# Moving both halves of the expert block's input by 32 bytes in SBUF

## The chip, the core and the metric

The kernel runs on one core of one Trainium2 chip. The metric is the device time of one execution in microseconds (us), lower is better. Before the change three runs took 735.52, 736.44 and 738.17 us; their median, 736.44 us, is what the changed kernel is compared with.

## The reference

Attention with a narrow window feeds a gated feed-forward block. Cut to what matters:

```python
batch, n_heads, seq, head_dim = (4, 8, 768, 64)
n_tokens, d_model, d_ff = (3072, 512, 1536)

scores = scale * q @ k.T - slope[h] * dist       # kept: 8 global columns, 96 local ones
a = softmax(where(keep, scores, -1e9))
x = (a @ v).transpose(0, 2, 1, 3).reshape(B * S, H * D)      # 3072 x 512
gate = 1.0 / (1.0 + np.exp(-(x @ w_gate)))
val = x @ w_val
return (gate * val @ w_out).astype(np.float32)
```

All of it is float32 in and float32 out.

## The kernel before, in words

**Tiling.** The 3072 tokens are cut into 8 blocks of 384 (three tiles of 128). For each block the kernel first makes x, transposed, with the 512 model dimensions on 4 x 128 partitions and the 384 tokens along the free dimension. Then it goes through the 12 slices of 128 hidden units (`seq`, line 631): `ff_in` (line 554) multiplies x by a slice of w_gate and of w_val, and `ff_out` (line 588) multiplies the result by the matching 128 rows of w_out and adds into three PSUM banks.

**Two halves.** TensorE multiplies here in a rounded 32-bit form (float32r). To keep float32 accuracy, each operand is split into a high half, which is the value rounded to that form, and a low half, which is the rest; a product is then three matmuls (low x high, high x low, high x high). x is kept as `xh` and `xl`, the first-layer weights as `w1h` and `w1l`, the second-layer weights as `w2h` and `w2l`, the hidden values as `hh` and `hl`.

**The matmuls that read x.** In `ff_in`, line 564, the weights are the stationary operand and x is the moving one:

```python
for wt, xt in ((w1l, xh), (w1h, xl), (w1h, xh)):
    nc.tensor.matmul(
        ps[:, :n], wt[f][:, i, c], xt[:, c, :n], start=(k == 0), stop=(k == 3 * NC - 1)
    )
```

That is 2 (gate, value) x 4 (chunks `c` of 128 dimensions) x 3 = 24 matmuls of 128 x 384 for one slice, and with 12 slices and 8 blocks 2304 in all. In `ff_out`, line 604, the hidden values are stationary and `w2l` or `w2h` is moving: 9 matmuls of 128 x 512 for one slice. The first six slices of the first block do `ff_out` in plain float32 instead.

**Who writes x.** `pair_out` (line 515) writes x for one pair of heads: for the first block three pairs by GpSimd (lines 540 and 541, the latter recorded under line 180, the helper `sub`), everything else by ScalarE (`xh`, line 544) and VectorE (`xl`, line 545). Each of `xh` and `xl` holds two blocks, one being read while the next is written.

**Order.** The attention of later blocks is cut into events (line 632) that are placed by hand between the slices of the expert block, so TensorE gets its attention work (lines 387 and 502) between `ff_in` and `ff_out`. A few orders are fixed by hand with `issue_after` (line 62). Nothing there names x's address.

**Where tiles lie.** A pool lays its tiles one behind the other in each partition, every tile rounded up to 32 bytes, and pools lie one behind the other in the order in which they are made (lines 45 to 50: wpool, cpool, xpool, small, mpool, w2pool). In the kernel before, counted in bytes from the start of a partition:

```
tile                          pool     starts at   modulo 64
w1h, w1l (24 tiles)           wpool    1152 ...    0
ident                         cpool    124128      32
xh                            xpool    131616      32
xl                            xpool    143904      32
sums, rcs, sm, rc, top, flag  small    156192 ...  32 and 0 in turn
gnm, gsm, grc                 small    156640 ...  32, 0, 32
work, hl, hh                  mpool    156736 ...  0
w2h, w2l                      w2pool   171072 ...  0
kr, pT, qs, ks                inner    175168 ...  0
```

The chunks of `xh` and `xl` lie 1536 bytes apart (384 x 4) and their two blocks 6144 bytes, both multiples of 64, so every slice of x that a matmul reads begins at 32 modulo 64.

**The branch that is not taken.** `dense_block` (line 794) is a general path for other values of n_global and n_local or for rows that don't fit; at the end a flag decides (`redo`, line 843), and line 845 runs in its place when it isn't needed. `gnm`, `gsm` and `grc` are used there alone.

Of the kernel before, what the change touches and what calls it, by code (L numbers as in the profile page):

```python
# [8 lines left out]
F32 = mybir.dt.float32  # L9
# [10 lines left out]
P = 128  # L20
# [8 lines left out]
def attn_moe_kernel(ctx, tc, qT, kT, v, n_global, n_local, wg, wv, wo, out, B, H, S, D):  # L29
# [17 lines left out]
    xpool = ctx.enter_context(tc.tile_pool(name="xpool", bufs=1))  # L47
    small = ctx.enter_context(tc.tile_pool(name="small", bufs=4))
# [218 lines left out]

    PAIR = 1
    blocks = [(b, t0, TB) for b in range(B) for t0 in range(0, NTB, TB)]
    xall = [xpool.tile([P, 2 * NC * NB], F32R, name=name) for name in ("xh", "xl")]  # L270
    xslot = {}
    offs = 0
# [496 lines left out]
    def dense_tables(t):  # L769
        reli = gpool.tile([P, S], I32, name="reli")  # L770
        nc.gpsimd.iota(reli, pattern=[[-1, S]], base=t * P, channel_multiplier=1)
        rel = gpool.tile([P, S], F32, name="rel")
        nc.vector.tensor_copy(rel, reli)
        keep = gpool.tile([P, S], F32, name="keep")
        pen = gpool.tile([P, S], F32, name="pen")
        dist = gpool.tile([P, S], F32, name="dist")
        nc.vector.tensor_scalar(keep, rel, nf[:, 0:1], None, op0=ALU.is_lt)
        nc.vector.tensor_scalar(pen, rel, 0.0, None, op0=ALU.is_ge)
        nc.vector.tensor_tensor(keep, keep, pen, op=ALU.mult)
        nc.gpsimd.iota(reli, pattern=[[1, S]], base=0, channel_multiplier=0)  # L780
        glo = gpool.tile([P, S], F32, name="glo")
        nc.vector.tensor_copy(glo, reli)
        nc.vector.tensor_scalar(glo, glo, nf[:, 1:2], None, op0=ALU.is_lt)
        nc.vector.tensor_tensor(pen, glo, keep, op=ALU.mult)
        nc.vector.tensor_tensor(glo, glo, pen, op=ALU.subtract)

        nc.vector.tensor_tensor(dist, rel, keep, op=ALU.mult)
        nc.vector.tensor_scalar(pen, glo, nf[:, 0:1], None, op0=ALU.mult)
        nc.vector.tensor_tensor(dist, dist, pen, op=ALU.add)
        nc.vector.tensor_tensor(keep, keep, glo, op=ALU.add)  # L790
        nc.vector.tensor_scalar(pen, keep, 1.0, 1.0e9, op0=ALU.subtract, op1=ALU.mult)
        return keep, pen, dist

    def dense_block(b, t0, xh, xl):
        for t in range(TB):
            keep, pen, dist = dense_tables(t0 + t)
            for s in range(NPAIR):
                r0 = b * (H * D) + 2 * s * D
                qg = gpool.tile([P, P], F32, name="qg")
                nc.sync.dma_start(qg, qT[bass.ds(r0, P), (t0 + t) * P:(t0 + t + 1) * P])  # L800
                kg = gpool.tile([P, S], F32, name="kg")
                nc.sync.dma_start(kg, kT[bass.ds(r0, P), :])
                vg = gpool.tile([P, NTB, P], F32, name="vg")
                nc.sync.dma_start(
                    vg, v[bass.ds(b * S, S), s * P:(s + 1) * P].rearrange("(t p) x -> p t x", p=P)
                )
                nc.vector.tensor_scalar(qg, qg, SCALE, None, op0=ALU.mult)
                av = ps_a.tile([P, 4 * P], F32, name="ps_v")
                for j in range(2):
                    hd = slice(j * D, (j + 1) * D)  # L810
                    sb = gpool.tile([P, S], F32, name="sb")
                    for c in range(S // NB):
                        cols = slice(c * NB, (c + 1) * NB)
                        ps = ps_gv.tile([P, NB], F32, name=("ps_g", "ps_u")[c % 2])
                        nc.tensor.matmul(ps, qg[hd], kg[hd, cols], start=True, stop=True)
                        nc.vector.scalar_tensor_tensor(
                            sb[:, cols], dist[:, cols], -slopes[2 * s + j], ps, op0=ALU.mult, op1=ALU.add
                        )
                    nc.vector.tensor_tensor(sb, sb, keep, op=ALU.mult)
                    nc.vector.tensor_tensor(sb, sb, pen, op=ALU.add)  # L820
                    nm = small.tile([P, 1], F32, name="gnm", bufs=1)
                    nc.vector.tensor_reduce(nm, sb, axis=AX.X, op=ALU.max, negate=True)
                    sm = small.tile([P, 1], F32, name="gsm", bufs=1)
                    nc.scalar.activation(sb, sb, AF.Exp, bias=nm, accum_out=sm)
                    nc.vector.tensor_scalar(sm, sm, 1e-9, None, op0=ALU.add)
                    rc = small.tile([P, 1], F32, name="grc", bufs=1)
                    nc.vector.reciprocal(rc, sm)
                    nc.vector.tensor_scalar(sb, sb, rc, None, op0=ALU.mult)
                    pT = gpool.tile([P, NTB, P], F32, name="gpT")
                    for c0 in range(0, NTB, 3):  # L830
                        pt = ps_a.tile([P, 4, P], F32, name="ps_t")
                        for c in range(3):
                            nc.tensor.transpose(pt[:, c], sb[:, (c0 + c) * P:(c0 + c + 1) * P], ident)
                        nc.scalar.copy(pT[:, c0:c0 + 3], pt[:, 0:3])
                    for c in range(NTB):
                        nc.tensor.matmul(
                            av[hd, 0:P], vg[:, c, hd], pT[:, c], start=(c == 0), stop=(c == NTB - 1)
                        )
                cols = slice(t * P, (t + 1) * P)
                nc.scalar.activation(xh[:, s, cols], av[:, 0:P], AF.Copy)  # L840
                nc.vector.tensor_tensor(xl[:, s, cols], av[:, 0:P], xh[:, s, cols], op=ALU.subtract)
# [4 lines left out]
    with fits.Else():  # L846
        with tc.For_i(0, B, 1) as b:
            for t0 in range(0, NTB, TB):
                blocks.append((b, t0, TB))
                bi = len(blocks) - 1  # L850
                xslot[bi] = (0, NC * NB)
                dense_block(b, t0, *x_of(bi))
                for f in range(NF):
                    split_w2(f)
                    ff_in(bi, f)
                    ff_out(bi, f)
# [39 lines left out]
```

## Time and profile before

| | |
|---|---|
| median of 3 runs (lowest to highest) | 736.44 us (735.52 to 738.17) |
| span of the profiled execution, first to last instruction | 734.4 us |
| matmul (PE) busy | 718.1 us, 98% of the span |
| weight loads (PEld) busy, beside the matmuls | 653.0 us, 89% |
| VectorE (DVE) / ScalarE (ACT) / GpSimd (POOL) busy | 498.8 / 420.2 / 219.4 us |
| mean granted TensorE clock | 0.998 of full speed |

The profile's time is a span from the first to the last instruction of one execution; the runs' times are measured around the whole execution, so the span is the smaller number (734.4 us against a median of 736.44 us). Busy times of the engines overlap. Matmuls are pipelined: the duration of one record (336 ns at the median for a matmul on x) is longer than the step from its start to the next one's start, and successive records overlap. The rate is read from starts, not from durations.

### The profile page before, as it was taken

To read this page: it belongs to the slowest core of one execution; us is meant where nothing else is said; L and a number is where in the kernel's file an instruction comes from. 1 tells how busy PE (TensorE), PEld (TensorE's weight loads), DVE (VectorE), ACT (ScalarE), POOL (GpSimd) and SP (SyncE) were. 2 spreads that over 40 slices of the span, in tenths; PEclk is the share of its full clock that TensorE was granted. 3 is DMA by queue.
4 is the path that set the end of the run, shared out by engine and by line. 5 is a ranking of instruction groups with operands and counts; after the bars stand their busy time and mean duration, and the time that the engine had idled before them with its cause. 6 is when DMAs were issued, how large, how long until landed. Compare 5 with 4: busy or idle time off the path is not lost. (4 is left out here: it accounts for less than half of the span.)

```text
span 734.4 us, 12477 instructions
## 1 busy us (share of the span) xinstructions
PE 718.1 (98%) x4403; PEld 653.0 (89%) x4403; DVE 498.8 (68%) x1303; ACT 420.2 (57%) x948; POOL 219.4 (30%) x166
## 2 busy tenths in 40 slices
PE   7999999999999999999999999999999999999996
PEld 5667788999889999999999999999999999999996
DVE  7889799668877777686777868666786877321111
ACT  5789887656565555566456655655555664332222
POOL 5424345422231323223132332313233231221222
PEclk9999999999999999999999999999999999999999
DMA  8969662624437353433435442343435224010001
GB/s 249 275 194 274 189 199 59 167 61 81 106 79 159 85 106 71 100 103 68 79 80 121 110 106 63 65 122 74 96 81 110 72 47 83 16 45 1 1 0 46
DMA packets 136866, 74.27 MB, mean 101 GB/s; under 512 B 87136, under 2 KB 129120, under 8 KB 136800
## 3 DMA queue, kind: packets, MB, share of 16 engines
q1 hardware_dynamic: 136800, 73.43, 40.1%
q8 instruction: 36, 0.59, 0.3%
q14 instruction: 30, 0.25, 0.1%
HBM read 49.81 MB, written 6.29 MB: 76 GB/s over the span
## 5 line engine op out<-in xcount | busy, mean ns | idle before, releaser
L180 POOL TENSOR_TENSOR w2l<-w2f,w2h 128x512 fp32r<-128x512 f32 x89 | 122.5, 1377 | 372.8 <-ACT w2h L217 359.1
L581 DVE SCALAR_TENSOR_TENSOR work<-work,ps_u 128x384 f32<-128x384 f32 x90 | 49.8, 553 | 127.1 <-PE ps_u L564 122.1
L564 PE MATMUL ps_g<-xh,w1l 128*128 128x384 f32 x384 | 131.1, 341 | 1.0 <-ACT work L572 1.0
L564 PE MATMUL ps_u<-xh,w1l 128*128 128x384 f32 x384 | 130.9, 341 | 0.1
L564 PE MATMUL ps_g<-xl,w1h 128*128 128x384 f32 x384 | 129.6, 337 | 0.7 <-DVE xl L545 0.7
L564 PE MATMUL ps_g<-xh,w1h 128*128 128x384 f32 x384 | 129.4, 337 | 0.0
L564 PE MATMUL ps_u<-xh,w1h 128*128 128x384 f32 x384 | 129.3, 337 | 0.0
L564 PE MATMUL ps_u<-xl,w1h 128*128 128x384 f32 x384 | 129.2, 336 | 0.0
L584 ACT ACTIVATE hh<-work 128x384 fp32r<-128x384 f32 x90 | 46.9, 521 | 131.3 <-DVE work L581 131.1
L419 ACT ACTIVATE work<-work,nms 128x256 f32<-128x256 f32 (+1 forms) x192 | 92.0, 481 | 25.8 <-DVE nms L406 25.4
L604 PE MATMUL ps_o<-w2l,hh 128*128 128x512 f32 x267 | 104.9, 393 | 0.6 <-POOL w2l L180 0.5
L604 PE MATMUL ps_o<-w2h,hh 128*128 128x512 f32 x267 | 104.1, 390 | 0.0
L604 PE MATMUL ps_o<-w2h,hl 128*128 128x512 f32 x267 | 103.1, 389 | 0.0
L180 DVE TENSOR_TENSOR hl<-work,hh 128x384 fp32r<-128x384 f32 x90 | 79.6, 884 | 23.4 <-ACT hh L584 23.2
L217 ACT ACTIVATE w2h<-w2f 128x512 fp32r<-128x512 f32 x89 | 56.0, 630 | 52.3 <-PE ps_o L604 51.0
L564 PEld LDWEIGHTS ps_g<-xh,w1l 128*128 128x128 f32 x384 | 72.2, 188 | 5.1 <-issue 2.3
L564 PEld LDWEIGHTS ps_u<-xh,w1l 128*128 128x128 f32 x384 | 72.1, 188 | 3.9 <-issue 1.2
L564 PEld LDWEIGHTS ps_g<-xl,w1h 128*128 128x128 f32 x384 | 72.2, 188 | 2.6 <-DVE xl L545 1.1
L564 PEld LDWEIGHTS ps_u<-xl,w1h 128*128 128x128 f32 x384 | 72.2, 188 | 1.0
L438 DVE TENSOR_SCALAR work<-work,rc 128x256 f32<-128x256 f32 (+1 forms) x168 | 71.4, 464 | 2.0
L564 PEld LDWEIGHTS ps_g<-xh,w1h 128*128 128x128 f32 x384 | 72.2, 188 | 0.5 <-issue 0.2
L564 PEld LDWEIGHTS ps_u<-xh,w1h 128*128 128x128 f32 x384 | 72.2, 188 | 0.0
(133 smaller groups left out, 1170.0 us busy)
## 6 DMA issues: line engine op xcount, KB each, us to landing
qr<-in_qT SPq DMA_DIRECT2D x56, 192.0 KB, 3.3
kr<-in_kT SPq DMA_DIRECT2D x32, 192.0 KB, 2.7
v<-in_v SPq DMA_DIRECT2D x32, 192.0 KB, 3.6
raw<-in_w_gate SPq DMA_DIRECT2D x12, 512.0 KB, 4.3
raw<-in_w_val SPq DMA_DIRECT2D x12, 512.0 KB, 5.6
raw<-in_w_out SPq DMA_DIRECT2D x12, 512.0 KB, 3.8
out<-ost SPq DMA_DIRECT2D x24, 256.0 KB, 2.2
v<-in_v SPq DMA_DIRECT2D x16, 144.0 KB, 3.8
```

Of the source, the lines that this page charges most:

```text
L180: eng.tensor_tensor(out, a, b, op=ALU.subtract)
L217: ins = nc.scalar.activation(hi, w, AF.Copy)
L419: ins = nc.scalar.activation(sb[:, j, :w], sb[:, j, :w], AF.Exp, scale=-1.0, bias=nm[:, j:j + 1], accum_out=sm[:, j:j + 1])
L438: nc.vector.tensor_scalar(sb[:, j, :w], sb[:, j, :w], rc[:, j:j + 1], None, op0=ALU.mult)
L564: nc.tensor.matmul(ps[:, :n], wt[f][:, i, c], xt[:, c, :n], start=(k == 0), stop=(k == 3 * NC - 1))
L581: nc.vector.scalar_tensor_tensor(a[:, :n], a[:, :n], 1.0, pss[1][:, :n], op0=ALU.add, op1=ALU.mult)
L584: nc.scalar.activation(hh[:, :n], a[:, :n], AF.Copy)
L604: ins = nc.tensor.matmul(outs[bi][t], ht[:, t * P:(t + 1) * P], wt, start=(f == 0 and k == 0), stop=(f == NF - 1 and k == len(parts) - 1),)
```

## The change

A tile of 8 floats (32 bytes) that nothing writes or reads is made in xpool ahead of `xh` and `xl`. In `dense_block` the tiles `gnm` and `grc` get one common slot, which makes the pool `small` 32 bytes shorter. So `xh` starts at 131648 and `xl` at 143936, both multiples of 64; the tiles of `small` lie 32 bytes further as well (up to the end of that pool), and mpool and everything behind it starts where it did.

```diff
     blocks = [(b, t0, TB) for b in range(B) for t0 in range(0, NTB, TB)]
+    xpool.tile([P, 8], F32, name="xgap")
     xall = [xpool.tile([P, 2 * NC * NB], F32R, name=name) for name in ("xh", "xl")]
...
-                    nm = small.tile([P, 1], F32, name="gnm", bufs=1)
+                    nm = small.tile([P, 1], F32, name="gnm", tag="gnm", bufs=1)
                     nc.vector.tensor_reduce(nm, sb, axis=AX.X, op=ALU.max, negate=True)
                     sm = small.tile([P, 1], F32, name="gsm", bufs=1)
                     nc.scalar.activation(sb, sb, AF.Exp, bias=nm, accum_out=sm)
                     nc.vector.tensor_scalar(sm, sm, 1e-9, None, op0=ALU.add)
-                    rc = small.tile([P, 1], F32, name="grc", bufs=1)
+                    rc = small.tile([P, 1], F32, name="grc", tag="gnm", bufs=1)
                     nc.vector.reciprocal(rc, sm)
```

No instruction is added, removed or moved.

## Rows read from the trace of the kernel before

**Rows 1.** The page: busy time of each engine, and the granted clock in 40 slices.
```profile
PE 718.1 (98%) x4403; PEld 653.0 (89%) x4403; DVE 498.8 (68%) x1303; ACT 420.2 (57%) x948; POOL 219.4 (30%) x166
...
PEclk9999999999999999999999999999999999999999
```

**Rows 2.** Busy time by stretch; each engine's us and instructions, then clock, DMA share, GB/s.
```profile
0.00:60.00 60.00, 51.73 (x368) 37.99 (x369) 48.32 (x155) 43.58 (x109) 26.49 (x36) 1.00 0.79 239
60.00:150.00 90.00, 89.32 (x527) 74.74 (x527) 76.32 (x149) 69.94 (x136) 39.03 (x26) 1.00 0.58 173
150.00:600.00 450.00, 448.25 (x2765) 420.49 (x2764) 331.94 (x908) 260.72 (x613) 125.46 (x84) 1.00 0.41 91
600.00:700.00 100.00, 100.00 (x602) 93.73 (x601) 36.13 (x82) 37.09 (x76) 21.84 (x16) 1.00 0.13 27
```

**Rows 3.** Groups of PE: first and last of six on x, then w2.
```profile
L564 PE MATMUL ps_g<-xh,w1l 128*128 128x384 f32 x384 | 131.1, 341 | 1.0 <-ACT work L572 1.0
...
L564 PE MATMUL ps_u<-xl,w1h 128*128 128x384 f32 x384 | 129.2, 336 | 0.0
...
L604 PE MATMUL ps_o<-w2h,hh 128*128 128x512 f32 x267 | 104.1, 390 | 0.0
```

**Rows 4.** PE in order of time, two whole slices: start us, us, engine, line, operands.
```profile
630.17 0.34 PE L564 MATMUL ps_g<-xh,w1l 128*128 128x384 f32 x1
...
634.34 0.39 PE L604 MATMUL ps_o<-w2l,hh 128*128 128x512 f32 x1
...
636.38 0.34 PE L564 MATMUL ps_g<-xh,w1l 128*128 128x384 f32 x1
...
640.54 0.39 PE L604 MATMUL ps_o<-w2l,hh 128*128 128x512 f32 x1
...
642.59 0.34 PE L564 MATMUL ps_g<-xh,w1l 128*128 128x384 f32 x1
```

**Rows 5.** PE in order of time, a run of score matmuls, then w2.
```profile
400.13 0.63 PE L387 MATMUL ps_s<-ks,qs 128*128 128x256 f32 x4
400.60 0.39 PE L604 MATMUL ps_o<-w2l,hh 128*128 128x512 f32 x1
```

**Rows 6.** PE in order of time, two runs of plain float32 matmuls of 128 columns.
```profile
29.29 1.31 PE L502 MATMUL ps_v<-pT,v 128*64 128x128 f32 x20
...
31.12 0.88 PE L528 MATMUL ps_o<-ident,rcs 128*64 128x128 f32 x12
```

**Rows 7.** Groups of PE: one record of those two runs takes, in the mean.
```profile
L502 PE MATMUL ps_v<-pT,v 128*64 128x128 f32 x344 | 21.7, 274 | 1.6 <-DVE pT L455 1.6
...
L528 PE MATMUL ps_o<-ident,rcs 128*64 128x128 f32 x48 | 3.5, 281 | 0.0
```

**Rows 8.** Groups of ACT: x written from PSUM, and the gate written from PSUM.
```profile
L572 ACT ACTIVATE work<-ps_g 128x384 f32<-128x384 f32 x96 | 46.4, 483 | 35.5 <-PE ps_g L564 35.3
...
L544 ACT ACTIVATE xh<-ps_t 128x384 fp32r<-128x384 f32 x16 | 7.8, 489 | 9.0 <-PE ps_t L502 9.0
```

**Rows 9.** Groups of DVE: gate times value, and xl.
```profile
L581 DVE SCALAR_TENSOR_TENSOR work<-work,ps_u 128x384 f32<-128x384 f32 x90 | 49.8, 553 | 127.1 <-PE ps_u L564 122.1 <-ACT work L572 3.6 <-PE ps_s L387 1.1
...
L545 DVE TENSOR_TENSOR xl<-ps_t,xh 128x384 fp32r<-128x384 f32 x16 | 8.8, 547 | 3.1 <-ACT xh L544 3.1
```

**Rows 10.** PE's waits for data: waited for, us in total, times, longest.
```profile
PE ps_g L564 <- ACT work L572: 1.0, 2, 0.6
...
PE ps_g L564 <- DVE xl L545: 0.7, 1, 0.7
```

**Rows 11.** The small tiles rc and sm on DVE: duration ns min/median/max.
```profile
L436 DVE RECIPROCAL rc<-sm x84: 142/166/169, 40.0 to 624.0; 128x2 f32<-128x2 f32 x84
L434 DVE TENSOR_SCALAR sm<-sm x72: 155/169/1272, 135.9 to 623.8; 128x2 f32<-128x2 f32 x72
```

**Rows 12.** The last piece of the chain that ended last.
```profile
729.53 0.06 DVE top L845
```

## The prediction

> **What bounds the kernel now.** I read the busy times first: matmuls fill 98% of the span and no other engine passes 68%, with the clock granted in full in every slice [rows 1]. The stretches come next: from 60 to 700 us PE is busy for 89.32 + 448.25 + 100.00 = 637.6 of 640 us [rows 2]. So in that stretch TensorE is the bound. Nothing hides a nanosecond added to or taken off a matmul there, and work on another engine counts only where PE waits for it. Third, the groups of PE: the six kinds of matmul on x have 384 records each, 6 x 384 = 2304, the largest share of PE's work [rows 3]. Their 336 to 341 ns are no rate, because records overlap; the rate is the step from start to start. That is the fourth view, PE in order of time [rows 4]: the 24 matmuls on x go from 630.17 to 634.34 us and, one slice later, from 636.38 to 640.54 us, together 8.33 us for 48 steps, or **173.5 ns each**. The nine on w2 take 2.04 and 2.05 us, together 4.09 us for 18 steps, or **227.2 ns each**.
>
> At the upper of the clock's two levels, 2.4 GHz, which is what is granted there, 384 columns take 160.0 ns and 512 take 213.3 ns. So a matmul on x, which begins 32 bytes past a multiple of 64, takes 13.5 ns more than its columns need. A matmul on w2, whose moving and stationary operands both begin at a multiple of 64, takes 13.9 ns more. This comparison carries the prediction: the excess is there, but the aligned stream has it too.
>
> **The change part by part.**
>
> *x 32 bytes further, read by TensorE.* No row shows a float32r matmul on x at a multiple of 64, so its price is bounded by the aligned streams. The nearest is w2: same engine, same number form, directly behind x in the same slice. If x took over its excess, each step would grow by 13.9 - 13.5 = 0.4 ns, 2304 x 0.4 = 0.9 us **slower**. The other aligned stream is the scores, 256 columns of ks: four go from 400.13 to 400.60 us [rows 5], 117.5 ns each, which is 10.8 ns over their 106.7. A line through 10.8 ns at 256 columns and 13.9 at 512 gives 12.35 at 384, and x lies 1.15 ns above it: 2304 x 1.15 = 2.6 us **faster**. I take zero. Between the two ends w2 is the nearer row, and its 0.4 ns is less than rows rounded to 10 ns can tell: one such rounding over 18 steps is 0.6 ns. The ks run is only four long and has a change of operands at either end.
>
> One pair of rows compares the two starts at equal width. In plain float32, 20 matmuls move pT, which lies at a multiple of 64, and 12 move ident, which lies 32 past one [rows 6]. Less the last record's duration [rows 7], the steps are (1310 - 274) / 19 = 54.5 ns and (880 - 281) / 11 = 54.5 ns. A 32-byte offset costs nothing there. It is another number form, so this supports the zero and doesn't prove it.
>
> The Trainium skill speaks for a gain (TensorE: Matmul & The Clock Gate, "Back-to-back issue gap"): isolated matmuls at full clock follow each other by their columns over 2.4 GHz plus 2.5 ns, which for 384 columns is 162.5 ns. By that estimate a matmul on x loses 11 ns somewhere, and if alignment were the cause the change would bring 2304 x 11 = 25 us. The trace disagrees with that use of the rule: w2 is aligned and is as far above it.
>
> *x 32 bytes further, written by ACT, DVE and POOL.* An ACT write of xh takes 489 ns, a write of the same shape from PSUM into an aligned tile 483 [rows 8]; xl on DVE takes 547 ns, a two-operand instruction of that shape on aligned tiles 553 [rows 9]. So 6 ns either way; 8 blocks of 4 pairs make 32 writes of each half, 64 x 6 ns = 0.4 us, and PE waited for xl only once, for 0.7 us [rows 10]. The cover is that x is written ahead of the block that reads it. If the cover were gone, the whole price would be that 0.4 us. POOL writes three pairs in the first block, under the same lead. I take zero.
>
> *The small tiles 32 bytes further.* Slots of sums, rcs, sm and rc alternate between 32 past and at a multiple of 64 before and after; the shift only swaps which is which. Four rotating slots of rc give a median of 166 ns and a maximum of 169 [rows 11], so neither start is slower. Zero.
>
> *gnm and grc in one slot.* Could add a wait in `dense_block` alone. The chain that ended last closes with line 845 [rows 12], the branch that runs in its place. Zero. No queue, DMA or semaphore of the executed path is named in the diff, and nothing is moved past anything on SP or POOL.
>
> The sum is 0 on a span of 734.4 us. The median of the runs, 736.44 us, lies 2.0 us above that span, which I leave as it is: **736.4 us**.
>
> **The rivals.**
>
> *An aligned stream's excess grows with its columns (faster).* If what TensorE loses were per column, w2's 13.9 / 512 = 0.0271 ns would make 10.4 ns at 384, and x would be paying 3.1 ns for its offset: 2304 x 3.1 = 7.1 us, 729.3 us. For it: ks with half of w2's columns has less excess, 10.8. Against it: half of 13.9 would be 7.0, so the excess is nearer to a constant than to a share. Chance 0.08.
>
> *The offset is the whole excess (faster).* 2304 x 13.5 = 31.1 us, 705.3 us. This is the rule's gain above, priced by the rows. Against it stands the aligned w2 with 13.9. Chance 0.03.
>
> *The two reads of TensorE meet (slower).* Now x starts in the other half of a 64-byte unit than w1, which TensorE loads while x streams; after the change both start at its beginning. If two reads in step hinder each other, the price is paid in ff_in, on PE, and what decides is whether a step grows by over 1 ns (2.2 us / 2304). The dearest row with both operands at a multiple of 64 is ks with qs: 10.8 / 256 = 0.042 ns a column, 16.2 at 384, 2.7 more than now: 2304 x 2.7 = 6.2 us, 742.6 us. Against it: w2 with hh and hl has both at a multiple of 64 too, and pays 13.9. Chance 0.09.
>
> *The change doesn't do what it says.* An unused tile could be given no room, or a slot could be rounded otherwise; then x, or what lies behind it, isn't where the diff puts it. The time would be today's, 736.4 us. Chance 0.02, inside "same".
>
> **How the numbers follow.** My forecast has 0.78. A measurement here can tell about 0.3%, 2.2 us, from no change. Same is 0.78 + 0.02 = 0.80, faster 0.08 + 0.03 = 0.11, slower 0.09. The range takes the bounds of x's price and the spread of the runs: 736.44 - 2.6 - 0.9 (median to lowest run) = 732.9, and 736.44 + 0.9 + 1.7 (median to highest) = 739.0. It leaves out the three rivals that move the time, 0.20.
>
> **What would show it.** In a whole slice of the changed kernel near 630 us the 24 matmuls on x should again take 4.16 to 4.17 us and the nine on w2 2.04 to 2.05 us. PE's busy time from 60 to 700 us should stay at 637 to 638 us, the ACT and DVE writes of x within 10 ns of 489 and 547. The prediction is wrong if x's step leaves 172.5 to 174.5 ns: near 170.5 it is the rival by columns, near 160 the whole excess, near 176 the meeting of reads. If x's step holds and the time still moves by more than 2.2 us, the cause lies in an order or a wait that I held to be untouched.

## The result and the profile after

The change made the kernel **slower**: 741.77 us (median of 6 runs, 741.01 to 745.36) against 736.94 us for the kernel before in the same measurement (6 runs, 735.52 to 738.19), a ratio of 1.0071 with a 95% interval from 1.0052 to 1.0090. (The ratios here are the recorded ones, with intervals; they are not quotients of the two medians, which would be 1.0066 in this case.) The span of the profiled execution went from 734.4 to 739.6 us, 5.2 us more. Forecast were 736.4 us and "same" at 0.80.

The page of the changed kernel and its table of stretches, to be held against [rows 1] and [rows 2] (its source lines are numbered one higher, L565 for L564):

```profile
PE 725.6 (98%) x4403; PEld 658.1 (89%) x4403; DVE 500.2 (68%) x1303; ACT 420.4 (57%) x948; POOL 218.9 (30%) x166
...
PEclk9999999999999999999999999999999999999999
```

```profile
0.00:60.00 60.00, 53.41 (x366) 39.20 (x366) 49.02 (x155) 43.92 (x111) 26.96 (x36) 1.00 0.81 244
60.00:150.00 90.00, 89.66 (x526) 74.99 (x526) 76.13 (x149) 69.45 (x134) 38.61 (x25) 1.00 0.57 170
150.00:600.00 450.00, 448.34 (x2743) 419.39 (x2743) 331.32 (x902) 259.51 (x610) 123.63 (x83) 1.00 0.40 90
600.00:700.00 100.00, 100.00 (x600) 93.63 (x599) 37.08 (x87) 37.59 (x76) 21.86 (x16) 1.00 0.14 30
```

Read by shares, nothing has happened: PE is at 98% in both, the clock is granted in full, the instruction counts are the same, and from 60 to 700 us PE is busy for 638.0 us where it was busy for 637.6. A saturated engine that has become slower looks just as saturated. The count of matmuls shows it. In 450 us from 150 us on there were 2765 matmuls in 448.25 busy us, 162.1 ns for each; now there are 2743 in 448.34, 163.4 ns, 0.8% more. Up to 700 us the sums of the four rows are 4262 matmuls before and 4235 after. So the changed kernel is 27 matmuls behind at that point, 4.4 us at 163 ns each, of the 5.2 us by which it ends later.

The durations of the records show little of it. The groups of the changed kernel that answer to [rows 3] have means 1 to 2 ns above those before; over all groups it is 0 to 1 ns on x and 1 to 4 ns on w2, and as successive records overlap, none of this is a rate:

```profile
L565 PE MATMUL ps_g<-xh,w1l 128*128 128x384 f32 x384 | 131.2, 342 | 1.1 <-ACT work L573 1.1
...
L605 PE MATMUL ps_o<-w2h,hh 128*128 128x512 f32 x267 | 104.7, 392 | 0.0
```

The rate is in the starts. PE in order of time in the changed kernel, the two slices that answer to [rows 4] (start us, us, engine, line, operands):

```profile
634.51 0.34 PE L565 MATMUL ps_g<-xh,w1l 128*128 128x384 f32 x1
...
638.70 0.40 PE L605 MATMUL ps_o<-w2l,hh 128*128 128x512 f32 x1
...
640.76 0.34 PE L565 MATMUL ps_g<-xh,w1l 128*128 128x384 f32 x1
...
644.96 0.40 PE L605 MATMUL ps_o<-w2l,hh 128*128 128x512 f32 x1
...
647.02 0.34 PE L565 MATMUL ps_g<-xh,w1l 128*128 128x384 f32 x1
```

The 24 matmuls on x take 4.19 and 4.20 us (before 4.17 and 4.16), the nine on w2 2.06 and 2.06 us (before 2.04 and 2.05). The two slices take 12.51 us where they took 12.42. Both runs became longer, although w2, hh and hl lie exactly where they did. Over the whole trace, taking every pair of successive starts within a run that is not broken by a wait, the mean step on x went from 173.8 to 175.4 ns and on w2 from 227.6 to 230.4 ns. With 2304 and 810 matmuls that makes 3.7 + 2.2 = 5.9 us, a little more than the 5.2 us seen.

The steps are not all a little longer. This is one run on w2 in the changed kernel, its first, fifth and following starts:

```profile
687.92 0.40 PE L605 MATMUL ps_o<-w2l,hh 128*128 128x512 f32 x1
...
688.85 0.39 PE L605 MATMUL ps_o<-w2h,hh 128*128 128x512 f32 x1
...
689.98 0.34 PE L565 MATMUL ps_u<-xh,w1l 128*128 128x384 f32 x1
```

The first four steps take 0.93 us, 232 ns each; the last five take 1.13 us, 226 ns each, which is the step of the kernel before. So a disturbance comes in with the end of the run on x, and here it dies away after four matmuls. In other slices of the same trace it doesn't:

```profile
677.44 0.34 PE L565 MATMUL ps_u<-xh,w1l 128*128 128x384 f32 x1
...
681.68 0.40 PE L605 MATMUL ps_o<-w2l,hh 128*128 128x512 f32 x1
```

This run on x takes 4.24 us, 176.7 ns a step, and its steps are long to the end.

What lies beside a matmul is seen when weight loads (PEld) are shown as well. The kernel before, in order of time:

```profile
684.99 0.34 PE L564 MATMUL ps_u<-xh,w1l 128*128 128x384 f32 x1
684.99 0.19 PEld L564 LDWEIGHTS ps_u<-xl,w1h 128*128 128x128 f32 x1
685.16 0.34 PE L564 MATMUL ps_u<-xl,w1h 128*128 128x384 f32 x1
685.16 0.19 PEld L564 LDWEIGHTS ps_u<-xh,w1h 128*128 128x128 f32 x1
```

The weights of the next matmul begin to load when the present one begins to stream x (the same start to 10 ns). TensorE reads two tiles side by side: the moving one and the next stationary one.

### The profile page after: what moved, and what is told of

Its sections match the earlier page's. It is cut to its first block, busy times and chain, and to the rows that moved or that the text cites. A ratio compares the mean times of both kernels' runs of the same rounds, so it can differ in the third digit from the quotient of the medians.

```text
span 739.6 us, 12477 instructions
## 1 busy us (share of the span) xinstructions
PE 725.6 (98%) x4403; PEld 658.1 (89%) x4403; DVE 500.2 (68%) x1303; ACT 420.4 (57%) x948; POOL 218.9 (30%) x166
## 5 line engine op out<-in xcount | busy, mean ns | idle before, releaser
L565 PE MATMUL ps_g<-xh,w1l 128*128 128x384 f32 x384 | 131.2, 342 | 1.1 <-ACT work L573 1.1
L565 PE MATMUL ps_u<-xh,w1l 128*128 128x384 f32 x384 | 131.1, 341 | 0.0
L565 PE MATMUL ps_g<-xl,w1h 128*128 128x384 f32 x384 | 129.8, 338 | 0.7 <-DVE xl L546 0.7
L565 PE MATMUL ps_u<-xh,w1h 128*128 128x384 f32 x384 | 129.6, 337 | 0.0
L565 PE MATMUL ps_g<-xh,w1h 128*128 128x384 f32 x384 | 129.6, 337 | 0.0
L565 PE MATMUL ps_u<-xl,w1h 128*128 128x384 f32 x384 | 129.3, 337 | 0.0
L565 PEld LDWEIGHTS ps_g<-xh,w1l 128*128 128x128 f32 x384 | 72.1, 188 | 5.2 <-issue 2.8
L565 PEld LDWEIGHTS ps_u<-xh,w1l 128*128 128x128 f32 x384 | 72.0, 187 | 3.8 <-issue 1.2
L439 DVE TENSOR_SCALAR work<-work,rc 128x256 f32<-128x256 f32 (+1 forms) x168 | 73.2, 474 | 2.0
L565 PEld LDWEIGHTS ps_g<-xl,w1h 128*128 128x128 f32 x384 | 72.1, 188 | 2.6 <-DVE xl L546 1.1
L565 PEld LDWEIGHTS ps_u<-xl,w1h 128*128 128x128 f32 x384 | 72.0, 188 | 1.0
L565 PEld LDWEIGHTS ps_g<-xh,w1h 128*128 128x128 f32 x384 | 72.0, 188 | 0.5 <-issue 0.2
L565 PEld LDWEIGHTS ps_u<-xh,w1h 128*128 128x128 f32 x384 | 72.0, 187 | 0.0
```

The costliest lines, as they stand in the source:

```text
L439: nc.vector.tensor_scalar(sb[:, j, :w], sb[:, j, :w], rc[:, j:j + 1], None, op0=ALU.mult)
L565: nc.tensor.matmul(ps[:, :n], wt[f][:, i, c], xt[:, c, :n], start=(k == 0), stop=(k == 3 * NC - 1))
```

## The experiments

Three theories stood at first. **Place theory:** x at a multiple of 64 is slow by itself. **Meeting theory**, later widened to the **distance theory:** the two reads that run side by side hinder each other, and what counts is the distance between their addresses. **Small-tile theory:** not x but the shifted small tiles or the shared slot cost the time.

Four distances matter to the second, here as bytes modulo 256 in the kernel before: x to w1 is 131616 - 1152 = 130464 = 509 x 256 + 160, so 160; w2 to hh and hl is 0; across the seams, x to hh (the last matmul on x streams while hh is loaded) is 224 and w2 to w1 is 192. Chunks, halves, slices and alternating buffers of these tiles are multiples of 256 apart, so each distance is one number for the whole kernel. In the table, "x run" and "w2 run" are the 24 and the 9 steps of a slice between 660 and 718 us, where no attention is left; two values mean that both occur.

```
run                  x-w1 w2-hh x-hh w2-w1  x run us     w2 run us    ratio (95%)
before                160    0   224   192   4.17         2.04         1
after                 192    0     0   192   4.19, 4.24   2.05 - 2.08  1.0071 (1.0052 - 1.0090)
e1  small tiles only  160    0   224   192   4.17         2.04         0.9997 (0.9974 - 1.0020)
e2  w1 +32, x +32     160    0     0   160   4.17         2.08         1.0036 (1.0011 - 1.0062)
e3  w1 +32, x +64     192    0    32   160   4.20, 4.24   2.04 - 2.09  1.0049 (1.0030 - 1.0069)
e4  x +64             224    0    32   192   4.19         2.06         1.0041 (1.0019 - 1.0063)
e5  all tiles +32     160    0   224   192   4.17         2.04         0.9983 (0.9955 - 1.0011)
e6  x, behind +128     32    0   224    64   4.23         2.04, 2.09   1.0053 (1.0031 - 1.0074)
e7  xl +32            160*   0   224   192   4.21         2.05 - 2.08  1.0067 (1.0046 - 1.0089)
e8  after, again      192    0     0   192   4.19, 4.24   2.05 - 2.08  1.0071 (1.0048 - 1.0093)
e9  x, behind +512    160    0   224   192   4.17         2.04         0.9983 (0.9964 - 1.0001)
e10 x, behind +256    160    0   224   192   4.17         2.04         1.0010 (0.9995 - 1.0024)
e11 w2, behind +32    160   32   224   224   4.16, 4.24   2.09, 2.10   1.0073 (1.0050 - 1.0095)
e12 x, behind +32     192    0   224   224   4.16, 4.24   2.05, 2.09   1.0045 (1.0022 - 1.0068)
e13 w1 +32            128    0   224   160   4.22         2.04, 2.08   1.0078 (1.0050 - 1.0107)
e14 behind x +32      160    0   192   224   4.23         2.05, 2.09   1.0065 (1.0042 - 1.0088)

* xh alone; xl lies at 192
```

The four are not independent: x-w1 is x-hh less w2-hh plus w2-w1, modulo 256 (224 - 0 + 192 = 416 = 256 + 160). So none of them can be changed alone by moving x, w1, w2 or the hidden values as a whole; e7, which moves one half of x, is the exception.

**e1, the change without x.** A gap of 32 bytes ahead of the small tiles, the shared slot kept, x where it was.

```diff
+    small.tile([P, 8], F32, name="sgap", bufs=1)
...
-                    rc = small.tile([P, 1], F32, name="grc", bufs=1)
+                    rc = small.tile([P, 1], F32, name="grc", tag="gnm", bufs=1)
```

> x stays 32 bytes past a multiple of 64; only the small tiles lie 32 bytes further and gnm and grc share a slot, as in the change. Place theory (what counts is where x begins): nothing of the change's cost is left, about 737 us, x steps 173.4 to 173.9 ns, w2 steps near 227. Small-tile theory (the shifted small tiles or the shared slot cost the time): about 742 us, x steps near 175.4, w2 near 230.

PE in order of time, where a run on w2, a run on x and the next run on w2 begin:

```profile
683.51 0.39 PE L605 MATMUL ps_o<-w2l,hh 128*128 128x512 f32 x1
...
685.55 0.34 PE L565 MATMUL ps_u<-xh,w1l 128*128 128x384 f32 x1
...
689.71 0.39 PE L605 MATMUL ps_o<-w2l,hh 128*128 128x512 f32 x1
```

2.04 and 4.16 us, as before, and 0.9997 in time (0.9974 to 1.0020). The small tiles and the shared slot have nothing of the loss; the whole change is x's 32 bytes.

**e2 and e3, x against w1.** A gap ahead of w1 moves w1 and x together (e2); with another one ahead of x, both lie 32 bytes past a multiple of 64 (e3; gnm, gsm and grc then share one tile, so that mpool stays).

```diff
+    wpool.tile([P, 8], F32, name="wgap")
     w1h = [wpool.tile([P, 2, NC, P], F32R, name=f"w1h{f}") for f in range(NF)]
...
+    xpool.tile([P, 8], F32, name="xgap")      # e3
```

> x at a multiple of 64 as in the change, but w1h, w1l, w2f and the tables lie 32 bytes past one. Place theory (x alone counts): about 742 us, x steps near 175.4. Meeting theory (x and the weights that TensorE loads meanwhile hinder each other where both begin in the same half of 64 bytes): they are in different halves again, about 737 us, x steps near 173.8.

> Both w1 and x lie 32 bytes past a multiple of 64. Place theory: x is where it was modulo 64, about 737 us. Meeting theory: both in the same half, as in the changed kernel, about 742 us, x steps near 175.4 and w2 steps near 230.

In e2, x is at a multiple of 64 as in the change, and its steps are those of before: 173.6 ns in the mean.

```profile
683.23 0.34 PE L565 MATMUL ps_u<-xh,w1l 128*128 128x384 f32 x1
...
687.40 0.40 PE L605 MATMUL ps_o<-w2l,hh 128*128 128x512 f32 x1
...
689.47 0.34 PE L565 MATMUL ps_u<-xh,w1l 128*128 128x384 f32 x1
```

4.17 us on x, but 2.07 on w2 (230.9 ns a step in the mean). e3 has x where it was modulo 64, and x's steps are long, 175.1 ns. So the place theory fails twice, and on x's steps the meeting theory holds so far. That the distance of x to w1 alone decides them isn't shown by this pair, as x-hh and w2-w1 differ too; e11, e12 and e14 below show that it does not. And the time of e2, 741.06 us against 738.26 for the kernel before in the same measurement, lies between those of the two theories: the meeting theory, as put, had nothing that makes w2 slow. In e2 both distances inside the runs are those of before, and only those across the seams differ.

**e4, 64 bytes in place of 32.** As the change, with a gap of 16 floats (and gnm, gsm and grc in one tile, so that mpool stays).

> x moved by 64 bytes instead of 32, so it is again 32 past a multiple of 64 (96 past one of 128). Place and meeting theory with a unit of 64 bytes: about 737 us, x steps near 173.8. If the unit is 128 bytes or the mere shift counts: another time, about 742 us if any shift costs.

741.06 us, 1.0041: a unit of 64 bytes fails. x's steps were 174.2 ns, near those of before, and w2's 229.6.

**e5, everything together.** The gap ahead of w1 and nothing that takes the 32 bytes back.

> Every tile of the kernel lies 32 bytes further than before: x begins at a multiple of 64, w1, w2, hh, hl, qs and ks begin 32 past one; all distances between tiles are those of before. Distance theory (TensorE's two reads, moving operand and next weights, hinder each other according to the distance between their addresses): as before, about 737 us, x steps 173.8, w2 steps 227.6 ns. Place theory (a multiple of 64 for x costs by itself): about 742 us, x steps near 175.4.

```profile
681.74 0.39 PE L605 MATMUL ps_o<-w2l,hh 128*128 128x512 f32 x1
...
683.78 0.34 PE L565 MATMUL ps_u<-xh,w1l 128*128 128x384 f32 x1
...
687.95 0.39 PE L605 MATMUL ps_o<-w2l,hh 128*128 128x512 f32 x1
```

2.04 and 4.17 us, mean steps of 173.8 and 227.6 ns, a ratio of 0.9983. x begins at a multiple of 64, like in the change, and nothing is lost. (This profile's span is 739.3 us; its granted clock was 0.91 over the first 60 us. The rows shown are from a stretch at full clock.)

**e6, e9 and e10, how far until it repeats.** A gap of 128, 512 and 256 bytes ahead of x, and everything behind x goes along.

```diff
+    xpool.tile([P, 32], F32, name="xgap")     # e6; 128 in e9, 64 in e10
     xall = [xpool.tile([P, 2 * NC * NB], F32R, name=name) for name in ("xh", "xl")]
```

> x and everything behind it lie 128 bytes further, w1 stays. Distance theory with a unit of 128 bytes or less: the distances repeat, about 737 us, x steps 173.8, w2 steps 227.6. Distance theory with a larger unit: other steps, 738 to 743 us. Place theory: x is again 32 past a multiple of 64, about 737 us.

> x and everything behind it lie 512 bytes further, w1 stays (128 bytes cost 0.5%). Distance theory with a unit of 512 bytes (the length in bytes of one weight row that is loaded): distances repeat, as before, about 737 us, x steps 173.8 ns, w2 steps 227.6. A larger unit, or no repeating at all: other steps, 739 to 743 us.

> The same with 256 bytes. Distance theory with a unit of 256: as before, 737 us. With a unit of 512: other steps, x near 174 to 176, w2 near 229 to 231, 739 to 743 us.

e6, a run on x, one on w2, and the next on x:

```profile
682.80 0.34 PE L565 MATMUL ps_u<-xh,w1l 128*128 128x384 f32 x1
...
687.03 0.40 PE L605 MATMUL ps_o<-w2l,hh 128*128 128x512 f32 x1
...
689.12 0.34 PE L565 MATMUL ps_u<-xh,w1l 128*128 128x384 f32 x1
```

e10, a run on w2, one on x, and the next on w2:

```profile
684.74 0.39 PE L605 MATMUL ps_o<-w2l,hh 128*128 128x512 f32 x1
...
686.78 0.34 PE L565 MATMUL ps_u<-xh,w1l 128*128 128x384 f32 x1
...
690.95 0.39 PE L605 MATMUL ps_o<-w2l,hh 128*128 128x512 f32 x1
```

128 bytes cost 0.53% (4.23 and 2.09 us), 512 and 256 bytes nothing (4.17 and 2.04 us). So of the shifts tried, 32, 64 and 128 bytes change the time and 256 and 512 don't: the distances count modulo 256 bytes, 64 columns of 4 bytes.

**e7, one half alone.** The gap lies between xh and xl.

```diff
+    xpool.tile([P, 8], F32, name="xgap")      # behind xh, ahead of xl
```

> Only xl goes to a multiple of 64, xh stays 32 past one; 8 of the 24 matmuls on x in a slice read xl. If each matmul pays for its own operand's place: a third of the change's 1.6 ns, x steps near 174.3, only the steps around xl long, w2 steps as before near 227.6, about 738.5 us. If a disturbance carries on from one matmul to the next ones: steps of xh and of w2 grow too, x near 175 and w2 near 229 to 231, 740 to 742 us.

A run on w2 and one on x in e7 (its source lines are numbered two higher than before, L566 for L564):

```profile
683.48 0.39 PE L606 MATMUL ps_o<-w2l,hh 128*128 128x512 f32 x1
...
685.54 0.34 PE L566 MATMUL ps_u<-xh,w1l 128*128 128x384 f32 x1
...
689.75 0.39 PE L606 MATMUL ps_o<-w2l,hh 128*128 128x512 f32 x1
```

1.0067, as dear as the whole change, though 16 of the 24 matmuls on x read a tile that did not move. The run on x takes 4.21 us and that on w2 2.06; the mean steps are 175.6 and 230.1 ns. A third of the moved data gives the whole loss: what a disturbed matmul does is carried on to the next ones. This run also isolates one distance. The last matmul on x in a slice reads xh, so both seams are those of before, and w2-hh is too; xl against the weights inside the run is enough to start it. In the change x-hh differs as well, and what that adds isn't separated.

**e8, the change again.**

> The changed kernel once more, on the chip of e5 to e7. All theories: a ratio of about 1.007 to the kernel before, x steps near 175.4 and w2 steps near 230.4 ns. If the steps come out otherwise, what a layout costs is not fixed by the layout.

1.0071, mean steps 175.4 and 230.2 ns. A layout costs the same when it is measured again; e1, e5 and e9, which ran on three chips, have the same runs of 4.17 and 2.04 us.

**e11, another pair.** The gap lies ahead of w2h: x, w1, hh and hl stay.

> w2h, w2l and what lies behind them lie 32 bytes further; x, w1, hh and hl stay. Distance theory: the distance of w2 (moving) to hh and hl (loaded) changes, so w2's steps leave 227.6 ns (228 to 232), x's steps stay within 0.5 ns of 173.8, 737 to 741 us. If only x's place matters: as before in both, 737 us.

1.0073, with w2's steps at 233.1 ns, the longest of all. The expectation missed on the time (742.63 us against at most 741) and on x's steps: they rose by 0.8 ns to 174.6, where 0.5 was allowed. Two slices that follow each other show how:

```profile
683.82 0.34 PE L565 MATMUL ps_u<-xh,w1l 128*128 128x384 f32 x1
...
687.98 0.39 PE L605 MATMUL ps_o<-w2l,hh 128*128 128x512 f32 x1
...
690.08 0.33 PE L565 MATMUL ps_u<-xh,w1l 128*128 128x384 f32 x1
...
694.32 0.39 PE L605 MATMUL ps_o<-w2l,hh 128*128 128x512 f32 x1
```

The run on x takes 4.16 us and then 4.24, with x and w1 where they were. It is the carrying on of e7 in the other direction, or the changed seam from w2 to w1; this run doesn't separate the two.

**e12, x's distance to w1 alone of those on x.** x and everything behind it go 32 bytes further.

> x and everything behind it lie 32 bytes further: the distance of x to w1 is that of the change, the distances of x to hh, hl and w2 are those of before. If x against w1 sets the steps on x: x steps near 175.4 as in the change, 740 to 742 us. If x against what lies behind it does: x steps 173.8, 737 us.

1.0045, and x's steps are 174.6 ns, neither 175.4 nor 173.8. The order of time shows why, in two slices that follow each other:

```profile
684.33 0.34 PE L565 MATMUL ps_u<-xh,w1l 128*128 128x384 f32 x1
...
688.57 0.39 PE L605 MATMUL ps_o<-w2l,hh 128*128 128x512 f32 x1
...
690.62 0.34 PE L565 MATMUL ps_u<-xh,w1l 128*128 128x384 f32 x1
...
694.78 0.40 PE L605 MATMUL ps_o<-w2l,hh 128*128 128x512 f32 x1
```

The run on x takes 4.24 us in one slice and 4.16 in the next, with the same distances, and so on in turn to the end. So x at 192 from w1 is not slow by itself (4.16 us is the undisturbed 173.3 ns a step). A run on x or w2 is short or long according to the state in which it is entered, and it hands its state on.

**e13 and e14, the two open questions.** Is the other party of x really the weights that are loaded? And can a seam alone start it? In e13 a gap ahead of w1 moves w1, and nf goes into wf's slot, so that from ident on nothing else moves. In e14 a gap lies ahead of the small tiles and everything behind goes along; w1 and x stay.

```diff
+    wpool.tile([P, 8], F32, name="wgap")                       # e13
-    nf = cpool.tile([P, 2], F32, name="nf")
-    wf = cpool.tile([P, 3, 2], F32, name="wf")
+    wf = cpool.tile([P, 4, 2], F32, name="wf")
+    nf = wf[:, 3]
...
+    small.tile([P, 8], F32, name="sgap", bufs=1)               # e14
```

> Only the expert weights w1h, w1l (and w2f, which TensorE reads in the first half of the first block alone) lie 32 bytes further; x, hh, hl, w2h, w2l and the attention's tiles stay, so that the distance of x to w1 is 128 in place of 160 modulo 256. If the weights that TensorE loads while x streams are the other party: steps change though x did not move, x 174 to 177 ns or w2 228 to 232, 738 to 743 us. If x is hindered by something else (hh, hl, w2, writes of other engines): as before, about 737 us, x 173.8, w2 227.6.

> w1 and x stay, everything behind x lies 32 bytes further, so x to w1 and w2 to hh and hl are as before and only the distances across (x streaming while hh is loaded at the end of a run, w2 streaming while w1 is loaded) change. If only the two reads of one matmul's own run count: as before, about 737 us. If a disturbance at the seam between the runs is carried on: first steps of a run longer, x near 173.6 to 175, w2 near 229 to 231, 738 to 742 us.

e13:

```profile
683.53 0.39 PE L605 MATMUL ps_o<-w2l,hh 128*128 128x512 f32 x1
...
685.57 0.34 PE L565 MATMUL ps_u<-xh,w1l 128*128 128x384 f32 x1
...
689.80 0.39 PE L605 MATMUL ps_o<-w2l,hh 128*128 128x512 f32 x1
```

e14:

```profile
680.68 0.40 PE L605 MATMUL ps_o<-w2l,hh 128*128 128x512 f32 x1
...
682.76 0.33 PE L565 MATMUL ps_u<-xh,w1l 128*128 128x384 f32 x1
...
684.88 0.34 PE L565 MATMUL ps_g<-xh,w1l 128*128 128x384 f32 x1
...
687.00 0.40 PE L605 MATMUL ps_o<-w2l,hh 128*128 128x512 f32 x1
```

In e13 x didn't move, and its run takes 4.23 us; the mean step is 175.9 ns, the longest on x of all runs, at 1.0078. So the loaded weights are the other party. That w1 meets the other engines' writes to hh, hl and work rather than x's reads is what e2 speaks against: w1 lies there as far from those tiles as in e13, and the run on x takes 4.17 us. Whether it is w1 against x or w1 against w2 at the seam, e13 by itself doesn't tell; e7 shows the first at work. In e14 both inner distances are those of before, only those across the seams differ, and both runs are long (4.24 and 2.08 us), at 1.0065. So a seam alone is enough, as e2 had shown for w2. The expectation put this into the first steps of a run; here the first 12 steps on x take 2.12 us and the last 12 again 2.12.

All five layouts with the four distances of before (e1, e5, e9, e10 and the kernel before) have its runs of 4.17 and 2.04 us; the change and the nine others lose 0.36 to 0.78%. How the four distances combine to give a layout its price isn't shown. None beats the kernel before, and there is little left to win: 173.3 and 226.7 ns are the steps of its undisturbed runs, and its means are 0.5 and 0.9 ns above, 2304 x 0.5 + 810 x 0.9 = 1.9 us, 0.26%.

What happens inside isn't shown either: that the two reads ask the same part of the memory at the same time is an argument from the common start of load and matmul, and no run looks at it.

## Why the prediction was wrong, point by point

**What bounds the kernel** was right: TensorE does, nothing hides what its steps lose, and the loss went into the time nearly whole (5.2 us of the 5.9 that the steps add up to).

**x read by TensorE** is the step that failed, "I take zero". Its ends were 2.6 us faster to 0.9 us slower; measured were some 5 us slower, by the steps 3.7 us on x and 2.2 on w2. Two things were wrong in it. First, it took the place of one operand modulo 64 as what can matter, and compared x (32) with w2 (0). The runs show that a place by itself does not matter (e5: everything 32 bytes further costs nothing) and that the distances between operands modulo 256 do (e6, e7, e10, e13). The row of w2 was a good reading: 13.9 ns over its columns at a multiple of 64, 13.5 for x. But it told only that both streams were undisturbed in the kernel before, x at a distance of 160 from its weights and w2 at 0. It said nothing about x at 192. Nor do 13.5 and 13.9 differ by alignment: undisturbed, both streams take 13.3 ns over their columns (173.3 - 160.0 and 226.7 - 213.3), and the rest is in the first steps of a run and in rows rounded to 10 ns. Second, the bounds were made from undisturbed streams alone, so their upper end could hold no disturbance, and the 2.2 us on w2, which does not move, had no term at all.

**The pair of plain float32 runs** was read rightly, as a mean step, but was no evidence on the other number form. The changed kernel's two rows give the same steps:

```profile
28.61 1.31 PE L503 MATMUL ps_v<-pT,v 128*64 128x128 f32 x20
...
30.44 0.88 PE L529 MATMUL ps_o<-ident,rcs 128*64 128x128 f32 x12
```

These steps were as long as before the change. Of the four tiles only rcs moved, with the small tiles, so that the distance of ident to rcs changed and nothing came of it; pT and v stayed.

**x written by ACT, DVE and POOL** was right. The groups of the changed kernel:

```profile
L545 ACT ACTIVATE xh<-ps_t 128x384 fp32r<-128x384 f32 x16 | 7.8, 489 | 9.0 <-PE ps_t L503 9.0
```

```profile
L546 DVE TENSOR_TENSOR xl<-ps_t,xh 128x384 fp32r<-128x384 f32 x16 | 8.8, 547 | 3.1 <-ACT xh L545 3.1
```

489 and 547 ns, to the nanosecond those of [rows 8] and [rows 9]. **The small tiles** and **the shared slot** were right: e1 has nothing of the loss.

**The rivals.** "The two reads of TensorE meet", at 0.09, is what happened in kind: the reads named, the engine, the sign, and a step longer by over 1 ns (1.6 measured). Its price of 6.2 us was near the 5 us by luck: it put 2.7 ns on each step on x and nothing on w2, where 1.6 ns on x and 2.8 on w2 were measured. Wrong in it was when they meet: not only where both begin in the same half of 64 bytes (in e6 x and w1 begin in different halves, as before the change, and 0.53% is lost), and not in ff_in alone. It was given 0.09 because w2 with hh and hl has both at a multiple of 64 and is undisturbed; that argument assumed a unit of 64 bytes, where 256 counts. The two faster rivals are out: in no layout did the run on x go below 4.16 us, 173.3 ns a step, so that the 13.3 ns over the columns were not alignment.

**The rule weighed for a gain.** By the estimate that the prediction made from the Trainium skill (TensorE: Matmul & The Clock Gate, "Back-to-back issue gap") the isolated step is 162.5 ns. No layout came near it, the shortest run on x having 173.3 ns a step, so it was rightly not used for a gain. The same page of the Trainium skill ("Step-by-step: what each phase is for") says that TensorE's two operands come through two independent read ports. If that meant that the reads cannot hinder each other, moving w1 alone could not change the steps on x; e13 measures 175.9 against 173.8 ns, and the measurement decides.

**What would show it** did show it: x's step left the stated 172.5 to 174.5 ns, for 175.4, beside the 176 that was put down for the meeting of reads. The other sign, PE's busy time from 60 to 700 us, could not show it: it stayed inside the stated 637 to 638 us while the time moved.

## What to carry to other kernels

Where TensorE is saturated with float32r matmuls, the bytes between the moving tile and the stationary tile that is loaded meanwhile, inside a run and across its seams, are worth trying as a tuning parameter: up to 0.8% in this kernel. Any edit that shifts a pool can spend it or win it back, so compare layouts with all distances kept before an edit's own effect is believed. Read a saturated engine by the steps between starts or by instructions in a stretch, since the busy share does not move (98% in both) and the record durations hardly do. And a row that shows two streams undisturbed bounds nothing about a third arrangement: the range needs an end for the disturbed one.

## What the runs showed that was not expected

The steps of float32r matmuls here depend on the distances between operands modulo 256 bytes and not on a shift of all addresses together (e5); layouts with the distances of before came out alike on three chips. They have memory: the state of one run passes through the seam into the next, so that tiles that did not move become slower (w2 in the change, 227.6 to 230.4 ns), a third of the moved data costs as much as all of it (e7), and one layout alternates between 4.16 and 4.24 us for the same 24 matmuls (e12; e11 does so too).
